# Gate and value products of a SwiGLU kernel: fifteen block products for 2x3x3 blocks in place of seven for 2x2x2

## The chip, the cores and the metric

The kernel runs on one core of a Trainium2 chip. The metric is the device time of one execution in microseconds (us); of the kernel before there are three such times and one profiled execution. The engines are PE (TensorE, matrix products, results in PSUM), DVE (VectorE), ACT (ScalarE), POOL (GpSimd) and SP (SyncE, which here only issues transfers). All data is 32-bit float; an f32 matmul leaves two records in the trace, called passes here.

## The reference

Attention with normalised q and k over 8 sequences of 448 tokens, 12 heads of 64, and behind it a feed-forward part with a SwiGLU. Cut to what matters:

```python
q_n, k_n = rmsnorm(q, g_q), rmsnorm(k, g_k)
attn = softmax(q_n @ k_n^T / sqrt(64))            # per batch and head, 448 x 448
x = concat_heads(attn @ v)                        # 3584 x 768
xn = x / rms(x) * rms_g
g, val = xn @ w_gate, xn @ w_val                  # w_gate, w_val: 768 x 1536
out = (g * sigmoid(g) * val) @ w_out              # w_out: 1536 x 768
```

The weights arrive as 64-bit floats and are turned into 32-bit ones on the chip. The change concerns the two products with `w_gate` and `w_val`, "gate/value" from here on.

## The kernel before

**Order.** `safe_scores` writes the order of the work out by hand: the operations of every engine run in the order in which the program emits them. The main loop goes over 48 pairs of heads, six for each sequence b. A pair has an attention block of seven steps (scores and weighted values on PE, exponentials on ScalarE, their sums on GpSimd), and between the blocks stand the norms, reductions and transposes of the next pairs. `fill` hands out feed-forward "items" from the list `todo` at set places between these: while sequence b is in attention, first the out-projection of b-2, then the gate/value products of b-1 (`begin`). One item is one or a few chains of matmuls with what follows them. `pe(fn)` emits an item and advances the count `now["t"]`; `after(n, fn)` puts an operation n counts later. `LEFT` items at the end of the list are kept for the first block of the next sequence, which hands them out as 2, 1 and 1 around the norms of k. After the last attention block all that remains is emitted without attention work.

**Between two blocks.** `turn` transposes q and k on PE; ScalarE makes qT (L549) from the transposed q and VectorE copies kT (L550). The norms and squares of the next pairs (L530, L493) run on ScalarE in front of qT, their reductions on VectorE.

**Gate/value.** Sequence 0 is done directly (`plain`), while the weights are converted (`convert`) and stored to a DRAM scratch (`kept` for gate and value, `kept_o` for w_out). Sequences 1 to 7 use `quad`: x and the weights are cut into 2x2x2 blocks (224 tokens; inner dimension 384 = 3 chunks of 128; two halves of the columns), and for each of six column pairs of 128 gate and 128 value columns seven products in the order B11, T2, B21, T3, T1, T4, B22 take the place of eight. A product (`product`, matmul in L1081) is 2 (gate, value) x 3 chunks = 6 matmuls of 224 tokens, so a sequence has 252 and the program 1764. The left sides are the blocks A of x and their sums S1 to S4, made by VectorE in `norm_x` (list `slow`, one at a time). The right sides are the raw blocks B and the sums T1 to T4. The results are put together by `plus` (L1093, VectorE, PSUM plus SBUF), after one copy of the first by ScalarE (L1123); twice, a second product is added onto a bank in PSUM that has been read. `hand` makes silu(gate) * value: a tanh on ScalarE (L1100) and, one count later, two operations of VectorE (L1103, L1104, `rest`).

**Weights.** The T blocks are made once, in sequence 1: `derive` (L1003, VectorE) takes two raw blocks that have been loaded, `keep` stores the sum to `kept`, and later sequences load it. An item of column pair fp may not be emitted before all 8 (fp + 1) blocks of its pair and the ones before have been derived (the third number of an item, read in `fill`). `ask` issues the loads in the order of use on SP's queue, as soon as blocks in SBUF are free; there are 23 of them, `w`, and four, `top`, that the conversion leaves. `derive_o` (L1024) makes the 24 sums of w_out's blocks in the same stage, `derive_q` (L1051 to L1054) the two-level sums for the quad out-projection in sequence 2.

**Out-projection.** Sequences 1 and 4 use seven products with w_out (`out_strassen`), sequences 2, 3, 5, 6 and 7 a two-level scheme (`out_quads`), whose left sums are made by `left_q1` (L1248); some of its results are added by GpSimd (L1345). In PSUM the scores have four banks, `ps_m` one, the feed-forward part three (`ps_f`).

Of the kernel before, what the change touches and what calls it, by code (L numbers as in the profile page):

```python
# [25 lines left out]
BW = 384  # L26
# [309 lines left out]
def safe_scores(  # L336
# [25 lines left out]
    NW = 23  # L362
# [3 lines left out]
    x_pool, s_pool, slots = pool("c_x", 4), pool("c_xs", 3), pool("c_slots", 1)  # L366
# [245 lines left out]
    def x_of(g):  # L612

        b, hp = divmod(g, NPAIR)
        half, c = divmod(hp, 3)
        if c == 0 and ("x", b, half) not in st:
            st["x", b, half] = x_pool.tile([128, 3, S], F32, name="x")
        if hp == 0 and ("ss", b) not in st:
            st["ss", b] = tmp.tile([128, S], F32, name="ss", tag="ss", bufs=1)
        return st["x", b, half][:, c, :]  # L620
# [111 lines left out]
    def norm_x(b):  # L732
# [7 lines left out]
        xs = [st["x", b, h] for h in range(2)]  # L740

        def scale(hp):
            x = xs[hp // 3][:, hp % 3, :]
            nc.vector.scalar_tensor_tensor(x, x, rg[:, hp:hp + 1], ps[:, 0:S], ALU.mult, ALU.mult)
# [9 lines left out]
        a = st["left", b] = {f"A{r + 1}{h + 1}": xs[h][:, :, r * HT:(r + 1) * HT] for r in range(2) for h in range(2)}  # L754
        for h in range(2):
            st.pop(("x", b, h))

        def op(name, first, second, what):

            a[name] = a["A21"] if name == "S3" else s_pool.tile([128, 3, HT], F32, name="xs")  # L760
            nc.vector.tensor_tensor(a[name], a[first], a[second], what)

        slow.extend(lambda args=args: op(*args) for args in (("S1", "A21", "A22", ALU.add), ("S2", "S1", "A11", ALU.subtract),
                                                             ("S3", "A11", "A21", ALU.subtract), ("S4", "A12", "S2", ALU.subtract)))
# [4 lines left out]
    def hurry(jobs):  # L769
        while jobs:  # L770
            jobs.pop(0)()

# [10 lines left out]
    kept = scratch.tile([NFP, len(NAMES), 2, 128, BW], F32, name="kept")  # L783
# [18 lines left out]
    free_w = [slots.tile([128, BW], F32, name=f"w{i}") for i in range(NW)]  # L802
# [10 lines left out]
    def block():  # L813
        return free_w.pop(0), free_w

    def room(n):
        return len(free_w) >= n

    def give_back(key):
        t, home = st.pop(key)  # L820
        after(1, lambda: home.append(t))

    def data(key):
        return st[key][0][:, 0:BW]
# [7 lines left out]
    def split(raw, n):  # L832
# [4 lines left out]
        if n < 24 and n % 7 > 3:  # L837

            top = s_pool.tile([128, 3, HT], I32, name="xs")[:, 0:2].rearrange("p c n -> p (c n)")[:, 0:BW]
        else:  # L840
            top = cv_pool.tile([128, BW], I32, name="top")
# [13 lines left out]
    for fc in range(NFC):  # L855
        col, fp = divmod(fc, NFP)
        for w in range(2):
            for half in range(2):
                rows = (moe_w_gate, moe_w_val)[w][half * HALF:(half + 1) * HALF, fc * 128:(fc + 1) * 128]
                pieces.append((("w", 0, fp, BLOCKS[2 * col + half], w), rows.rearrange("(c p) f -> p c f", p=128)))  # L860
# [4 lines left out]
    turn_of = {"n": 0}  # L865
# [3 lines left out]
    def home(key):  # L869
        if key[0] == "w":  # L870
            return kept[key[2], NAMES.index(key[3]), key[4]]
# [5 lines left out]
    def keep(key):  # L877
        nc.sync.dma_start(out=home(key), in_=data(key))

    def convert():  # L880
# [18 lines left out]
        if turn_of["n"] == TURNS:  # L899

            free_w.extend(cv_pool.tile([128, BW], F32, name="top") for _ in range(4))
            whole = [raw_pool.tile([128, 2 * BW], F32, name="raw") for _ in range(7)]
            room_so.extend(whole[:6])
            homes = [whole[6][:, 0:BW], whole[6][:, BW:]] + [cv_pool.tile([128, BW], F32, name="top")[:, :] for _ in range(2)]
# [33 lines left out]
    def raw_q(b):  # L938
        n = sum(key[0] == "wx" for key in uses) // 2
        if n < len(jobs_q):  # L940
            i, j = jobs_q[n]
            uses.extend(("wx", b, ORDER_Q[i], c) for c in (j, j + KG))

    for b in range(1, B):
        for fp in range(NFP):
            for at, name in enumerate(("B12", "B11", "B22", "B21") if b == 1 else ORDER):
                uses += [("w", b, fp, name, w) for w in range(2)]
                if b == 2 and at % 4 == 1:
                    raw_q(b)
            if b == 1:  # L950
                uses += [("wd", b, name, fp) for name in BLOCKS]
        if in_quads(b):
            uses += stream_q(b)
        else:
            for name in ORDER_O:
                for c in range(NFP):
                    uses.append(("wo", b, name, c))
                    if b == 1 and c % 4 == 3 and name not in ORDER_O[:1]:
                        raw_q(2)
                    if b == 1 and c == 1 and name in ORDER_O[-3:]:  # L960
                        raw_q(2)
    assert sum(key[0] == "wx" for key in uses) == 2 * len(jobs_q)
    asked = {"n": 0, "derived": 0}
    derived = [(fp, to, plus, minus, w) for fp in range(NFP) for to, plus, minus in DERIVED for w in range(2)]

    def ask():

        if turn_of["n"] < TURNS:
            return
        while asked["n"] < len(uses):  # L970
            key = uses[asked["n"]]
            keep_free = 4
            if key[1] == 1 and key[0] in ("w", "wd"):
                fp = key[2] if key[0] == "w" else key[3]
                keep_free = max(7 + 8 * fp - asked["derived"], 1)
# [6 lines left out]
            if len(free_w) <= keep_free:  # L982
# [3 lines left out]
            st[key] = block()  # L986
# [3 lines left out]
    def derive(wait=4):  # L990
# [3 lines left out]
        fp, to, plus, minus, w = derived[asked["derived"]]  # L994
        for name in (plus, minus):
            if ("w", 1, fp, name, w) not in st or asked.get(("w", 1, fp, name, w), 0) > now["t"] - wait:
                return False
        if not free_w:
# [742 lines left out]
```

## Time and profile before

| | |
|---|---|
| three executions | 1542.72, 1543.2, 1545.05 us; median 1543.2 |
| profiled execution | 1546.19 us, its span 1544.4, granted clock 0.996 |
| VectorE, ScalarE, GpSimd busy | 60%, 35%, 48% of the span |
| PE, weighted values (L674), scores (L659) | 194.2 us, 233.8 us |
| PE, gate/value products of sequences 1 to 7 (L1081, four groups) | 69.5 + 45.9 + 344.4 + 265.2 us |
| transfers | 327.26 MB, mean 212 GB/s |

A row of a group reads: line, engine, operation, out<-in, shape, count | busy us, mean ns of one | idle us of that engine just before them, and what ended it. "x" and "xs" are the left blocks (raw and summed), "w" and "top" the right ones, "ff" a bank of `ps_f`. A row of the timeline has its start in the span, its length, engine and line, and in brackets the engine's idle time before it with what ended it; runs of like operations are put together (x12). In the windows each engine has its busy time with the number of instructions. Ends of matmuls are modelled by the profiler, so consecutive matmuls overlap in the records, and the time of one is better taken from the distance of starts.

### The profile page before, as it was taken

The numbers are of one execution on the slowest core, as the hardware profiler recorded it, in microseconds if no ns is written. First come the engines' busy times: TensorE is split into PE (matmuls) and PEld (weight loads), VectorE is DVE, ScalarE is ACT, GpSimd is POOL, SyncE is SP. The second block draws the span as 40 slices with busy tenths as digits, with TensorE's granted clock in tenths as the row PEclk, the third lists the DMA queues.
The fourth block names the chain that finished last, engine by engine and source line by source line (L and its number), as shares of the span: only waits on it lengthen the run. The fifth ranks groups of instructions, "written<-read, shape, count | busy, mean of one in ns | idle before, by whom it ended". The sixth has DMA issues, their size and how long they took to land.

```text
span 1544.4 us, 26111 instructions
## 1 busy us (share of the span) xinstructions
PE 1511.2 (98%) x8900; PEld 1187.4 (77%) x8900; DVE 929.8 (60%) x1793; ACT 534.8 (35%) x1241; POOL 736.4 (48%) x718
## 2 busy tenths in 40 slices
PE   8999998999999999999999999999999999999997
PEld 4344444688856888888987888767987889899997
DVE  5788998667754666854457443444458444673464
ACT  6856664333323333234233332424333232101000
POOL 6868887546424354474435652544545731030003
PEclk9999999999999999999999999999999999999998
DMA  7758575776989978886557855584557755577565
GB/s 194 228 153 258 175 228 157 225 229 214 294 274 275 310 253 266 285 250 188 160 163 217 267 176 153 152 275 131 174 155 228 240 160 148 164 256 256 175 194 176
DMA packets 314082, 327.26 MB, mean 212 GB/s; under 512 B 84308, under 2 KB 310868, under 8 KB 313940
## 3 DMA queue, kind: packets, MB, share of 16 engines
q1 hardware_dynamic: 313012, 325.31, 68.1%
q8 instruction: 73, 1.20, 0.3%
q14 instruction: 69, 0.57, 0.1%
q10 hardware_dynamic: 800, 0.20, 0.1%
q0 software_dynamic: 128, 0.00, 0.0%
HBM read 271.62 MB, written 53.77 MB: 211 GB/s over the span
## 4 chain that ended last, share of the span: by engine, by line
PE 83%; DVE 11%; DMA 2%; issue 1%; ACT 1%; POOL 1%; SPq 0%; DVEq 0%; POOLq 0%; ACTq 0%
PE ff L1081 42%; PE ff L1373 10%; PE sc L659 7%; PE av L674 6%; PE ff L1305 5%; PE ff L1440 4%; PE tr L544 2%; PE ff L1178 2%; DVE top L850 1%; DVE top L849 1%; PE den L692 1%; PE den L606 1%; DVE top L848 1%; PE sc L562 1%; DVE l L1248 1%
## 5 line engine op out<-in xcount | busy, mean ns | idle before, releaser
L1081 PE MATMUL ff<-x,w 128*128 128x224 f32 x1686 | 344.4, 354 | 0.0
L1081 PEld LDWEIGHTS ff<-x,w 128*128 128x128 f32 x1686 | 315.2, 190 | 13.2 <-issue 11.3
L1081 PE MATMUL ff<-xs,w 128*128 128x224 f32 x1296 | 265.2, 353 | 2.0 <-DVE w L1003 1.2
L714 POOL TENSOR_TENSOR es<-es,e 128x448 f32<-128x448 f32 x205 | 245.9, 1200 | 13.7
L1081 PEld LDWEIGHTS ff<-xs,w 128*128 128x128 f32 x1296 | 243.9, 190 | 3.4 <-issue 1.5
L659 PE MATMUL sc<-qT,kT 64*64 64x448 f32 x1176 | 233.8, 542 | 5.7 <-ACT e L664 2.9
L674 PE MATMUL av<-e,vt 64*64 64x448 f32 x984 | 194.2, 541 | 0.0
L664 ACT ACTIVATE e<-sc 128x448 f32<-128x448 f32 x294 | 154.4, 547 | 71.4 <-PE sc L659 53.5
L644 POOL TENSOR_TENSOR ss<-ss,rd 128x448 f32<-128x448 f32 x40 | 48.0, 1201 | 218.5 <-ACT rd L643 218.5
L659 PEld LDWEIGHTS sc<-qT,kT 64*64 64x64 f32 x1176 | 79.3, 133 | 87.4 <-issue 61.6
L709 POOL TENSOR_TENSOR es<-e 128x448 f32<-128x448 f32 x41 | 48.2, 1176 | 178.0 <-ACT e L664 178.0
L515 POOL TENSOR_TENSOR rs<-ms,mhalf 128x12 f32<-128x12 f32 (+1 forms) x50 | 115.9, 2319 | 4.2
L1093 DVE TENSOR_TENSOR cc<-ff,u 128x448 f32<-128x448 f32 x84 | 52.3, 623 | 99.6 <-PE ff L1081 99.5
L1440 PE MATMUL ff<-x,w 128*128 128x448 f32 x288 | 111.8, 541 | 0.0
L674 PEld LDWEIGHTS av<-e,vt 64*64 64x64 f32 x984 | 66.2, 133 | 42.4 <-issue 42.4
L1100 ACT ACTIVATE th<-c 128x224 f32<-128x224 f32 x42 | 16.3, 389 | 238.1 <-DVE c L1093 238.1
L1373 PE MATMUL ff<-w,l 128*128 128x192 f32 x500 | 95.6, 329 | 2.8 <-DVE l L1248 2.0
L1440 PEld LDWEIGHTS ff<-x,w 128*128 128x128 f32 x288 | 53.3, 190 | 51.1 <-issue 49.2
L1373 PEld LDWEIGHTS ff<-w,l 128*128 128x128 f32 x500 | 82.6, 190 | 8.1 <-DVE l L1248 3.2
L1345 POOL TENSOR_TENSOR y<-y,c 128x384 f32<-128x384 f32 x10 | 12.2, 1217 | 159.4 <-DVE y L1414 148.0
L1093 DVE TENSOR_TENSOR u<-ff,p 128x448 f32<-128x448 f32 x42 | 26.2, 623 | 84.3 <-PE ff L1081 77.9
L1093 DVE TENSOR_TENSOR u<-ff,u 128x448 f32<-128x448 f32 x42 | 26.1, 623 | 82.6 <-PE ff L1081 82.3
(209 smaller groups left out, 2627.9 us busy)
## 6 DMA issues: line engine op xcount, KB each, us to landing
w<-kept SPq DMA_DIRECT2D x474, 192.0 KB, 3.7
w<-kept_q SPq DMA_DIRECT2D x297, 192.0 KB, 3.8
w<-kept_o SPq DMA_DIRECT2D x132, 192.0 KB, 3.9
kept<-w SPq DMA_DIRECT2D x81, 192.0 KB, 3.9
top<-kept SPq DMA_DIRECT2D x78, 192.0 KB, 3.9
top<-kept_q SPq DMA_DIRECT2D x53, 192.0 KB, 3.2
kept_q<-w SPq DMA_DIRECT2D x52, 192.0 KB, 3.0
qk<-in_q_dram SPq DMA_DIRECT2D x48, 192.0 KB, 3.5
```

Source lines behind the costliest of these rows:

```text
L515: nc.gpsimd.tensor_tensor(st["rs", g][:, cols], ms, mhalf[:, cols], ALU.pow)
L644: after(m, lambda: (nc.gpsimd.tensor_tensor(ss, ss, rd, ALU.add), st.update({("summed", b): hp})))
L659: nc.tensor.matmul(ps[r, 0:S], lhsT=st["kT", g][r, keys_of(i)], rhs=st["qT", g][r, :], start=True, stop=True)
L664: nc.scalar.activation(e, ps[:, 0:S], ACT.Exp)
L674: nc.tensor.matmul(st["av", g][own(j), 0:S], lhsT=vt, rhs=st["e", g, i][r], start=i == 0, stop=i == PARTS - 1, skip_group_check=True)
L709: nc.gpsimd.tensor_tensor(st["es", g], st["e", g, 0], st["e", g, 1], ALU.add)
L714: nc.gpsimd.tensor_tensor(st["es", g], st["es", g], st["e", g, i], ALU.add)
L1081: nc.tensor.matmul(bank[:, w * HT:(w + 1) * HT], lhsT=wt[:, c * 128:(c + 1) * 128], rhs=x[:, c, :], start=onto is None and w == c == 0, st ...
L1093: nc.vector.tensor_tensor(add[name], ps[:, 0:S], add[other], ALU.add)
L1305: nc.tensor.matmul(ps, lhsT=left_o(b, which, LEFT_O[name], c), rhs=data(("wo", b, name, c)), start=first and c == 0, stop=c == NFP - 1, sk ...
L1373: nc.tensor.matmul(ps, lhsT=a[:, j, :], rhs=data(key)[:, n % 2 * HW:(n % 2 + 1) * HW], start=start and j == 0, stop=j == KG - 1, skip_grou ...
L1440: nc.tensor.matmul(bank[w][:, 0:S], lhsT=data(key)[:, c * 128:(c + 1) * 128], rhs=st["x", 0, half][:, c, :], start=half == c == 0, stop=ha ...
```

## The change

Gate and value of sequences 1 to 7 use fifteen products for 2x3x3 blocks (`three`): tokens 2 x 224, inner dimension 3 x 256 (2 chunks of 128), and a group of columns 3 x (128 gate + 128 value); there are four such groups, taken in the order 0, 2, 1, 3. The direct way has 18 products. A product is 2 x 2 = 4 matmuls of 224, a sequence 60 products.

```diff
+    LEFT_G = {"S3": ("a21", "a23", ALU.add), "S6": ("a23", "a22", ALU.subtract), "S8": ("a11", "a12", ALU.subtract),
+              "S9": ("a13", "a21", ALU.add), "S4": ("a13", "S6", ALU.subtract), "S5": ("a21", "S8", ALU.subtract),
+              "S2": ("a12", "S4", ALU.subtract), "S0": ("a22", "S5", ALU.subtract), "S1": ("a23", "a13", ALU.subtract),
+              "S13": ("a11", "a21", ALU.subtract), "S12": ("a11", "a13", ALU.add)}
+    RIGHT_G = {"v9": ("b11", "b33", None), "v4": ("b21", None, "b32"), "v5": ("b12", None, "b23"),
+               "v1": ("b21", "b33", "b31"), "v14": ("b12", "b21", "b22"), "v11": ("b22", "b23", "b32"),
+               "v10": ("b13", "b12", "-b33"), "v13": ("b13", "b11", "b23"), "v7": ("b31", "b11", "-b32")}
+    PRODUCTS = (("q3", "S3", "b33"), ("q6", "S6", "b32"), ("q8", "S8", "b12"), ("q9", "S9", "v9"), ("q4", "S4", "v4"),
+                ("q5", "S5", "v5"), ("q7", "a13", "v7"), ("q2", "S2", "b21"), ("q0", "S0", "b23"), ("q1", "S1", "v1"),
+                ("q14", "a12", "v14"), ("q11", "a22", "v11"), ("q12", "S12", "b11"), ("q10", "a21", "v10"), ("q13", "S13", "v13"))
```

Left sums: 11 operations of 448 per sequence in place of four of 672; one that isn't made yet is made in front of its product. The results are chained in three banks, B, X and Y: the next product is added onto a bank that ScalarE has copied out, without a new start. In the order of the products: q3 into B, q6 X, q8 Y, q9 onto B, q4 onto X, q5 onto Y, q7 B, q2 X, q0 Y, q1 B, q14 X, q11 Y; q12 into a new bank Z, q10 into another, q13 onto Z.

```diff
+        def copy(name, ps):
+            nc.scalar.copy(T[name], ps[:, 0:S])
+        def plus(name, ps):
+            nc.vector.tensor_tensor(T[name], ps[:, 0:S], T[name], ALU.add)
+        def more(name, one, other, what):
+            nc.gpsimd.tensor_tensor(T[name], T[one], T[other], what)
...
+        def q5(make):
+            T["pc"] = pair("pc")
+            T["c13"], T["c23"] = T["pc"][:, 0], T["pc"][:, 1]
+            copy("c13", make(bank["Y"]))
+            more("c13", "c13", "s", ALU.add)
+            more("c13", "c13", "d", ALU.subtract)
...
+        def q11(make):
+            plus("c22", make(bank["Y"]))
+            after(1, lambda: hand("pa", 1, 1))
+        def q12(make):
+            bank["Z"] = make()
+            plus("c11", bank["Z"])
+            after(1, lambda: hand("pb", 0, 2))
+        def q10(make):
+            ps = make()
+            plus("c23", ps)
+            plus("c13", ps)
+        def q13(make):
+            if n == len(GROUPS) - 1 and in_quads(b):
+                after(1, lambda: left_q1(b, 0, range(3)))
+            plus("c13", make(bank["Z"]))
+            after(1, lambda: hand("pc", 2, 1))
```

In each group ScalarE copies after q3, q6, q8, q9, q4, q5, q7, q2 and q0 (nine "snapshots", 252 in all; before, 42 copies), GpSimd makes five sums (140 in all), VectorE seven `plus` (196, before 210), and three `hand` of 448 each finish two column blocks of both token halves (84 tanh in place of 126).

Derived right blocks: nine per group, 15 operations of 512 (60 in all, before 48 of 384), one block per item, and an item may be emitted as soon as the block that it uses itself has been derived; so the derivation of a block may stand one or two items in front of its product. When all are made, `derive_o` runs twice per item, and the first item of a block name in the out-projection of sequence 1 forces what is still missing.

```diff
+    derived = [(g, to) for g in GROUPS for _, _, to in PRODUCTS if to in RIGHT_G]
...
+                made += b == 1 and right in RIGHT_G
+                items.append((4 * HT, TURNS, (made, ("wg", b, g, right)), fn))
...
+            made, key = sums_made or (0, None)
+            while asked["derived"] < made or (key and key not in st):
+                before = dict(asked)
                 derive(0)
+                if key and key[0] == "wo":
+                    derive_o(0)
                 ask()
-                if n == asked["derived"]:
+                if before == asked:
                     pe(idle)
...
             if now["t"] - st["block"] > 4 and now["t"] != st.get("left_sums"):
-                left = 3 - sum(derive() for _ in range(3))
-                for _ in range(left):
+                if not derive():
                     derive_o()
-                for _ in range(2):
-                    derive_q()
+                derive_o()
+                derive_q()
```

Weights in SBUF: a gate/value block is 128 x 512 (gate and value together, 256 KB). The 23 single blocks become an arena of 22 x 384 columns in places of 128; gate/value blocks take four places from its start, others three from its end, and 18 places are kept for the raw blocks of `derive_o` and `derive_q` (`side`, loaded in their own order) until `derive_q` is through. A load is issued only if more than three further blocks of its kind find room (two for the raw blocks of sequence 1).

```diff
+            kind, keep_free = "wg" if key[0] == "wg" else "w", 3
+            if key[1] == 1 and key[0] == "wg":
+                keep_free = 2
...
-            if len(free_w) <= keep_free:
+            if not room(keep_free + 1, kind):
                 return
```

Converted blocks of gate and value are stored as three pieces of 128 columns. In the quad out-projection the sum for B22 (ten operations of 384) goes from GpSimd to VectorE. The pools of x, its sums and the temporaries are cut anew. Since an item is smaller now, `LEFT` is 10 in place of 7, and they are handed out as 3, 2 and 1:

```diff
-    AHEAD, LEFT = 20, 7
+    LEFT = 10
...
+        fill(3)
+        norm_k(g + 1, 0)
         fill(2)
-        norm_k(g + 1, 0)
-        fill(1)
         pe(lambda: turn(g + 1, 0))
```

The program has 10507 matmuls where it had 10591; the other shapes of matmul keep their numbers. SP issues 1831 transfers in place of 1999.

## The prediction

> **What bounds the kernel now.** I read the page from the top, then the windows of the gate/value stages, then timelines around single products, then the groups by line and the waits of VectorE. First the page:
>
> ```profile
> PE 1511.2 (98%) x8900; PEld 1187.4 (77%) x8900; DVE 929.8 (60%) x1793; ACT 534.8 (35%) x1241; POOL 736.4 (48%) x718
> ...
> PE 83%; DVE 11%; DMA 2%; issue 1%; ACT 1%; POOL 1%; SPq 0%; DVEq 0%; POOLq 0%; ACTq 0%
> ...
> L1081 PE MATMUL ff<-x,w 128*128 128x224 f32 x1686 | 344.4, 354 | 0.0
> ...
> L1081 PE MATMUL ff<-xs,w 128*128 128x224 f32 x1296 | 265.2, 353 | 2.0 <-DVE w L1003 1.2
> ...
> w<-kept SPq DMA_DIRECT2D x474, 192.0 KB, 3.7
> ```
>
> TensorE is busy 98% of the span at a granted clock of 0.996, so work taken from it shortens the kernel only as far as no new wait appears. The two L1081 rows are the gate/value products; before them PE idled 2.0 us in all, 1.2 behind a derived block. Two smaller rows read blocks from another buffer; each f32 matmul leaves two records, so 1764 matmuls are 3528 passes.
>
> The windows show the stage of sequence 1, where the derived weights are made, and a stretch of the last stage with nothing but products:
>
> ```profile
> core 0: us, PE busy (x) PEld busy (x) DVE busy (x) ACT busy (x) POOL busy (x), PEclk, DMA share, GB/s
> 320.00:450.00 130.00, 128.83 (x772) 102.82 (x765) 92.10 (x183) 47.48 (x114) 65.04 (x58) 1.00 0.76 244
> 1400.00:1425.00 25.00, 25.00 (x134) 25.00 (x133) 8.24 (x17) 3.16 (x7) 0.00 (x0) 1.00 0.74 229
> ```
>
> In the second, a pass takes 25/134 = .187 us. Over all gate/value stages the median distance between starts of passes is .189, which I use. VectorE has 71% of the first stretch, the fullest of its stages.
>
> **Removed from TensorE.** 84 matmuls go, 168 passes: 168 × .189 = **−31.8**. By the mean of the busy time (69.5+45.9+344.4+265.2 = 725 us over 3528 passes, .2055, with overlaps counted twice) it is −34.5; by .1866, −31.3. A product is now 8 passes, 1.51 us, where it was 12, 2.27.
>
> **Work added to the others.** The rows that price it:
>
> ```profile
> L1003 DVE TENSOR_TENSOR w<-w,w 128x384 f32<-128x384 f32 x23 | 11.9, 549 | 0.0
> L1024 DVE TENSOR_TENSOR w<-w,w 128x384 f32<-128x384 f32 x22 | 15.4, 702 | 0.4
> L1103 DVE SCALAR_TENSOR_TENSOR h<-th,cc 128x448 f32<-128x448 f32 x42 | 26.4, 629 | 0.7 <-ACT th L1100 0.7
> L1104 DVE SCALAR_TENSOR_TENSOR h<-h,cc 128x448 f32<-128x448 f32 x42 | 27.1, 645 | 1.4
> L1123 ACT COPY p<-ff 128x448 f32<-128x448 f32 x42 | 22.4, 532 | 121.7 <-PE ff L1081 94.1 <-POOL c L1345 27.6
> L714 POOL TENSOR_TENSOR es<-es,e 128x448 f32<-128x448 f32 x205 | 245.9, 1200 | 13.7
> ```
>
> ScalarE: 210 more copies × .532 = +112, less 42 tanh × .389 or less. GpSimd: 140 adds × 1.20 = +168, less ten that move away. VectorE: 60 derived steps instead of 48; a 512-wide step I take at .68 (192 columns .35–.44, 384 .55–.70, so .16–.2 per further 128). By these counts VectorE goes from 956 to 979 us, ScalarE 598 to 705, GpSimd 746 to 903: none becomes the bound over the whole. In sequence 1's gate/value, PE falls from 126 to 122 us and VectorE rises from 93 to 109; that is cover enough on average, and the price comes from order, below.
>
> [...]
>
> ```profile
> L638 DVE TENSOR_TENSOR x<-av,rd 128x448 f32<-128x448 f32 x28 | 17.4, 621 | 2.2 <-PE av L674 1.1
> L638 DVE TENSOR_TENSOR x<-x,rd 128x448 f32<-128x448 f32 x20 | 17.3, 864 | 0.7
> ```
>
> (621 with one input in PSUM, 864 with both in SBUF.) [...]
>
> **Waits in sequence 1's gate/value.** Each derived block is now made one or two products ahead of its use, by VectorE, and behind operations that wait for TensorE themselves. Nothing else is in front of PE then: it stands, and with it the score matmuls queued behind. The timeline gives the handover:
>
> ```profile
> 549.13 0.62 DVE L1093 TENSOR_TENSOR cc<-ff,u 128x448 f32<-128x448 f32 x1
> 549.67 0.61 DVE L1093 TENSOR_TENSOR c<-ff,u 128x448 f32<-128x448 f32 x1
> ...
> 549.80 2.54 PE L1081 MATMUL ff<-xs,w 128*128 128x224 f32 x12 [0.80 <-DVE cc L1093]
> ...
> 552.38 0.62 DVE L1093 TENSOR_TENSOR cc<-ff,u 128x448 f32<-128x448 f32 x1 [1.63 <-PE ff L1081]
> ```
>
> The product that starts at 549.80 ends at 549.80 + 12 × .189 = 552.07; VectorE starts on it .31 later; a second 448-wide sum starts .54 after the first; PE follows the end of a VectorE sum (549.75) by .05.
> - First column group: four products in a row, each with a left sum (.61), a derived step (.68) and an out-projection sum (.70), ask VectorE 2.0 us against PE's 1.51. Worked through operation by operation, q9 waits 2.0 and q5 1.5.
> - First group, q13: its block v13 is emitted behind two sums on q10's result and the pair of the first `hand`: .31 + two sums 1.08 + pair (L1103, L1104) 1.27 + two dependent steps 1.40 + .05 = 4.1.
> - Second group, q13: the same, with the copy of kT (L550, which waits for qT, shown below) and reductions in front: 5.0.
> - Third group: q7 2.3, q11 3.2, and q10, q13 and the next q6 and q9 .4–.7 each, 2.3.
> - Fourth group: q14 1.2, q11 .7, q10 1.0, q13 .8: 3.7.
>
> Sum 24.1, less the 1.2 that is there already: **+23**. Low: only the two q13 and half of the rest, 12; high: the rest half as dear again and the 512-wide step at .86, 32.
>
> **Waits in the out-projection of sequence 1.** The blocks T2 of w_out are stored to DRAM and loaded back when all 24 sums are made. The last four (c=5) are now forced just in front of their first use. In front of them on VectorE stands the copy of kT, which waits for qT of ScalarE, which is behind three norms and two squares:
>
> ```profile
> DVE kT L550 <- ACT qT L549: 61.7, 33, 4.0
> ```
> ```profile
> 1058.61 0.81 ACT L530 ACTIVATE qk<-qk,rs 128x64 f32<-128x64 f32 x3
> ...
> 1059.32 0.93 ACT L493 ACTIVATE sq<-qk 128x384 f32<-128x384 f32 x2
> ...
> 1061.06 0.63 ACT L549 ACTIVATE qT<-tr,gqk 128x448 f32<-128x448 f32 x1 [0.81 <-PE tr L548]
> ```
>
> From the end of PE's work: .31 + a copy .48 + norms .7 + squares .8 + qT .6 = 3.0; reductions .9; four sums 2.0; store and issue .45; landing 3.0–3.9 (192 KB take 3.7 in the page's row): 9.4–10.2, less transposes of .9 that run meanwhile: **+9**. Low, without the queue in front: sums and landing, less what PE has left, 4.4. High: store and load after each other, 11.
>
> **Smaller ones.** Start of sequence 2's gate/value: its first block is asked for one product before use: landing 3.7 less 1.5, and issue behind the others 1.2: **+3.4** (1 to 6). Starts of out-projections of sequences 2, 3, 5, 6, 7: `left_q1` now stands behind the last pair of `hand` (1.27, of which .45 is hidden): **+4** (0 to 8). Chains in PSUM: the next product on a bank comes two products (3.02) after the last; a snapshot needs .31 + .53, so ScalarE's exps between may take 2.2 us before PE waits; where four exps of .55 stand in front it is even: **+1** (0 to 10). Loads: a gate/value block is 256 KB, fewer are held, and the shortest lead is 4.9–5.5 us at the starts of sequences 3, 4, 6, 7 against a landing of 3.7–3.9: **+3** (0 to 8).
>
> At nothing: the last sums of the quad out-projections (B22, ten of 384) go from GpSimd (1.22 each) to VectorE (.55), which has room there; two of them lie at the kernel's end, so −1.3 at best. `LEFT` 10 and the fills of 3, 2, 1 hand out 4.5, 3.0 and 1.5 us where 2, 1, 1 products of 2.27 were 4.5, 2.3 and 2.3: the same cover, and .8 less for the last turn if it were short. The stores of converted weights are three pieces of the same bytes.
>
> **Sum.** −31.8 + 23 + 9 + 3.4 + 4 + 1 + 3 = **+11.6**. Against the profiled execution (1546.19, span 1544.4 and 1.8 around it) 1557.8; that execution is 3 above the median, so **1555** by the median. All low ends: −34.5 + 12 + 4.4 + 1 = −17, 1526. All high ends: −31.3 + 32 + 11 + 6 + 8 + 10 + 8 = +44, 1587.
>
> **Rivals.**
> - *Faster, the waits stay short.* For: the one wait for a derived block that the trace has is small, 1.17 us:
>
> ```profile
> 361.71 1.37 PE L1081 MATMUL ff<-xs,w 128*128 128x224 f32 x6 [1.17 <-DVE w L1003]
> ```
>   Ten such places cost 12, the out-projection 4.4, the small ones 4: −31.8 + 20.4 = −11.4, **1532**. It decides from where sequence 1's gate/value waits less than 11.4 us in all (31.8 less the other terms as summed above, 9 + 3.4 + 4 + 1 + 3). Against: in that trace the block was not behind a sum of the product just before; here v13 is, every time.
> - *ScalarE's snapshots hold PE in every stage.* For: nine per group, 252 in all, each in front of a product on its bank. If 35 blocks of exps each cost .4, +14 to +15: **1570**. Against: ScalarE is 35% busy and gets 3.02 us.
> - *Transfers bind.* For: the DMA share is .76 already in sequence 1, and fewer blocks are held. Ten late loads of 1 us: +10, **1565**. Against: fewer transfers in number (1999 issues on SP's queue become 1831).
> - That TensorE's work does not fall can be left out: the program lists 10507 matmuls instead of 10591, the other shapes unchanged.
>
> **Chances.** My forecast (waits in sequence 1 and its out-projection eat the gain, 1541–1572) .52; faster .28; snapshots .12; transfers .08. About 0.2%, 3 us, is what a measurement of this kernel can tell from no change: that band (1540–1546) takes .06 of the forecast's low end and .01 of the first rival. So faster .28, same .07, slower .65. The range 1530–1576 leaves out the fast part of the first rival and the slow tail of the snapshots.
>
> **What would show it.** Products at .189 per pass with 168 passes fewer; in sequence 1, PE waits of 4–5 us before q13 of the first two groups, put down to VectorE's derived steps, and some 20 us of PE idle there; a wait of 9–10 us for a DMA at the first T2 product of its out-projection. Wrong, if the derived steps come out on time (VectorE waiting for blocks, not PE for VectorE), if PE idles instead before the products that follow a snapshot, or if its idle time lies at the starts of stages with a DMA named.

## The result, and the profile after

The changed kernel takes 1614.68 us (median of 4 runs, 1613.91 to 1617.44) beside 1543.05 of the kernel before: a ratio of 1.0465, 95% interval 1.0446 to 1.0483, 72 us slower. The profiled execution has a span of 1612.4 us, 68.0 more than before.

The page of the changed kernel:

```profile
PE 1508.5 (94%) x8732; PEld 1170.4 (73%) x8732; DVE 981.7 (61%) x1766; ACT 639.6 (40%) x1409; POOL 898.2 (56%) x848
...
PEclk9999999999988999999999999999999999999999
...
L1162 PE MATMUL ff<-x,w 128*128 128x224 f32 x1344 | 278.6, 362 | 20.5 <-DVE w L1075 12.4
...
L1183 POOL TENSOR_TENSOR pc<-pc,l 128x448 f32<-128x448 f32 x84 | 98.7, 1175 | 254.2 <-ACT pc L1177 231.2
...
w<-kept SPq DMA_DIRECT2D x396, 256.0 KB, 3.7
```

PE has 168 passes fewer and is busy 2.7 us less in a span 68 us longer: the time went into waiting and into slower work. The clock row has two slices of 8 where only the last one was below 9 before, at 443 to 524 us: the end of the stage in which the derived weights are made, and the out-projection behind it. The waits of VectorE, ScalarE and GpSimd do not matter by themselves; those of PE do. The list of PE's waits (line waited for, total, times, longest):

```profile
PE ff L1162 <- DVE w L1075: 26.2, 11, 6.7
PE ff L1425 <- DMA w<-kept_o: 9.4, 3, 8.5
PE ff L1496 <- issue: 8.7, 5, 2.0
PE msx L725 <- POOL ss L643: 7.7, 5, 1.9
PE ff L1162 <- DVE pb L1180: 7.5, 6, 1.5
```

L1075 is the second step of a derived block, L1425 the out-projection of sequences 1 and 4, L725 the matmul on the sums of squares in front of an out-projection, L1496 the quad out-projections, L1180 the `plus` of a gate/value group. The windows by stage (gate/value of sequence 1; its out-projection with the wait at the start of sequence 2; gate/value of 2, of 3, of 7):

```profile
294.10:460.10 166.00, 135.72 (x769) 112.75 (x767) 121.95 (x182) 60.56 (x134) 93.91 (x82) 0.91 0.52 168
460.10:545.50 85.40, 71.51 (x303) 38.58 (x303) 37.40 (x77) 18.50 (x43) 23.35 (x23) 0.94 0.64 200
545.50:679.40 133.90, 124.53 (x761) 105.18 (x762) 83.38 (x157) 57.64 (x125) 77.03 (x72) 0.98 0.92 287
746.60:867.60 121.00, 118.03 (x754) 101.19 (x754) 51.05 (x93) 57.18 (x124) 79.16 (x76) 1.00 0.58 179
1463.10:1552.40 89.30, 89.30 (x474) 89.30 (x473) 32.42 (x57) 24.67 (x46) 23.30 (x23) 1.00 0.66 201
```

The lengths, taken between the first products of each stage, before and after: 125.7 and 166.0; 67.7 and 85.4; 124.7 and 133.9; 121.3 and 121.0; 93.1 and 89.3. The first two stages of the kernel before, in the same form:

```profile
296.50:422.20 125.70, 124.53 (x793) 108.11 (x791) 91.22 (x176) 46.00 (x111) 69.40 (x64) 1.00 0.77 250
422.20:489.90 67.70, 67.70 (x304) 37.47 (x303) 36.78 (x84) 18.63 (x43) 23.63 (x24) 1.00 0.88 269
```

Where nothing but products runs (sequence 7) the gain of 3.8 is there; in sequence 3 it is used up; sequence 1 alone, with its out-projection, loses 58.

### The profile page after: what moved, and what is told of

It reads as the page before. It is cut to its first block, busy times and chain, and to the rows that moved or that the text cites. A ratio compares the mean times of both kernels' runs of the same rounds, so it can differ in the third digit from the quotient of the medians.

```text
span 1612.4 us, 25793 instructions
## 1 busy us (share of the span) xinstructions
PE 1508.5 (94%) x8732; PEld 1170.4 (73%) x8732; DVE 981.7 (61%) x1766; ACT 639.6 (40%) x1409; POOL 898.2 (56%) x848
## 5 line engine op out<-in xcount | busy, mean ns | idle before, releaser
L1162 PE MATMUL ff<-x,w 128*128 128x224 f32 x1344 | 278.6, 362 | 20.5 <-DVE w L1075 12.4
L1162 PEld LDWEIGHTS ff<-x,w 128*128 128x128 f32 x1344 | 258.1, 195 | 28.9 <-issue 10.2
L1183 POOL TENSOR_TENSOR pc<-pc,l 128x448 f32<-128x448 f32 x84 | 98.7, 1175 | 254.2 <-ACT pc L1177 231.2
L1162 PE MATMUL ff<-xs,w 128*128 128x224 f32 x896 | 181.5, 358 | 8.8 <-DMA w<-kept 4.7
L1162 PEld LDWEIGHTS ff<-xs,w 128*128 128x128 f32 x896 | 170.6, 194 | 13.9 <-issue 7.7
L1180 DVE TENSOR_TENSOR pb<-ff,pb 128x448 f32<-128x448 f32 x56 | 34.8, 621 | 189.7 <-PE ff L1162 187.0
L1496 PE MATMUL ff<-w,l 128*128 128x192 f32 x630 | 119.0, 330 | 14.7 <-issue 8.7
L1496 PEld LDWEIGHTS ff<-w,l 128*128 128x128 f32 x630 | 103.4, 190 | 22.0 <-issue 12.1
L1162 PE MATMUL ff<-top_x,w 128*128 128x224 f32 x448 | 93.0, 357 | 3.1 <-DVE w L1075 2.0
L1162 PEld LDWEIGHTS ff<-top_x,w 128*128 128x128 f32 x448 | 83.1, 190 | 15.2 <-issue 12.3
L1564 PEld LDWEIGHTS ff<-x,w 128*128 128x128 f32 x288 | 53.8, 192 | 51.6 <-issue 49.6
L1162 PE MATMUL ff<-l,w 128*128 128x224 f32 x448 | 89.7, 353 | 0.0
```

The source lines that it names most:

```text
L1162: nc.tensor.matmul(bank[:, w * HT:(w + 1) * HT], lhsT=data(key)[:, (2 * w + c) * 128:(2 * w + c + 1) * 128], rhs=a[left][:, c, :], start=o ...
L1180: nc.vector.tensor_tensor(T[name], ps[:, 0:S], T[name], ALU.add)
L1183: nc.gpsimd.tensor_tensor(T[name], T[one], T[other], what)
L1496: nc.tensor.matmul(ps, lhsT=a[:, j, :], rhs=data(key)[:, n % 2 * HW:(n % 2 + 1) * HW], start=start and j == 0, stop=j == KG - 1, skip_grou ...
L1564: nc.tensor.matmul(bank[w][:, 0:S], lhsT=data(key)[:, c * 128:(c + 1) * 128], rhs=st["x", 0][:, 3 * half + c, :], start=half == c == 0, st ...
```

## What a wait costs: the clock

Two windows of the stage of sequence 1, around and right behind the end of the first long wait:

```profile
330.00:337.00 7.00, 6.35 (x19) 5.77 (x20) 3.52 (x8) 1.81 (x5) 0.00 (x0) 0.52 0.36 123
337.00:344.00 7.00, 7.00 (x40) 6.95 (x40) 6.90 (x14) 2.75 (x6) 5.60 (x6) 1.00 0.47 174
```

PE is busy in both; in the first it does 19 passes at a granted clock of 0.52, in the second 40 at 1.00. The prediction has no term of this kind, so it was measured by itself, with waits put into the kernel before:

```diff
+        if (fp, right) == (3, "B21"):
+            for _ in range((0, 0, 1, 2, 3, 5, 8, 12)[b]):
+                nc.vector.tensor_scalar(x[:, :, 0:192], x[:, :, 0:192], 1.0, None, ALU.mult)
```

> The kernel before with one wait put into each of the sequences 2 to 7: 1, 2, 3, 5, 8 and 12 multiplications by 1.0 of VectorE on the left block of the product with B21 in column pair 3. Waits of some 1.7, 2.5, 3.3, 4.9, 7.3 and 10.5 us of TensorE, 30 in all. Theory 'a wait is paid twice': windows of half the granted clock follow the waits of about 3 us and more, 3.4 to 10 us long each, and the time grows by the waits plus 8 to 16: 1581-1590. Rival 'a wait costs what it lasts': no windows, 1543 + 30 = 1570-1576.

1592.5 us beside 1548.85 of the kernel before, one execution each. The waits of PE in the timeline ("issue": the profile names nothing; PE waits for the multiplications that were put in front of the product):

```profile
557.07 2.51 PE L1084 MATMUL ff<-x,w 128*128 128x224 f32 x12 [2.49 <-issue]
747.87 2.58 PE L1084 MATMUL ff<-x,w 128*128 128x224 f32 x6 [3.88 <-issue]
941.70 3.70 PE L1084 MATMUL ff<-x,w 128*128 128x224 f32 x9 [4.48 <-issue]
1117.73 2.58 PE L1084 MATMUL ff<-x,w 128*128 128x224 f32 x6 [7.32 <-issue]
1313.98 3.32 PE L1084 MATMUL ff<-x,w 128*128 128x224 f32 x8 [7.45 <-issue]
1485.44 2.95 PE L1084 MATMUL ff<-x,w 128*128 128x224 f32 x7 [9.02 <-issue]
```

| wait, us | stretch of half clock, us | stage longer by, us |
|---|---|---|
| 2.49 | none | 2.9 |
| 3.88 | 6.83 | 6.6 |
| 4.48 | 6.83 | 7.6 |
| 7.32 | 6.83 | 9.5 |
| 7.45 | 10.24 | 10.5 |
| 9.02 | 10.24 | 11.7 |

The waits sum to 34.6, the stages grow by 48.8 (the span by 46.3, as this execution reached sequence 1 2.5 us earlier). Here the wait of 2.49 us costs about what it lasts, those from 3.88 on 2 to 3 us more, about half of that part of the stretch which lies outside the wait. The stretches are two and three times 3.41 us long here, one to three times in the changed kernel. There a shorter wait was enough: one of 1.94 us and one of .61 just behind it were followed by 3.41 us of half clock.

The traces show more. In each of them the stretches start at whole multiples of 3.413 us from one another (in the changed kernel at 329.92, 370.88, 405.01, ...). If the time at full clock, from 290 us on to the last gate/value product, is cut into pieces on this grid, the 14 profiles have 4904 of them. All 60 in which PE has 2.0 us or more without a matmul record are followed by half clock, 17 of the 53 with 1.5 to 2.0 us are, and 1 of the 4791 with less. The wait of 2.49 us lies across a border of the grid, .54 on one side and 1.95 on the other; waits of 1.97 and 1.71 that fall into one piece almost whole were followed by half clock in the changed kernel.

From the start of sequence 1's gate/value to the last of the gate/value products the changed kernel has 54.6 us of such stretches, the kernel before none. 10.8 us of them lie within waits; the other 43.8 at half speed are an estimate of 22 us lost.

## Why PE waits in sequence 1

The first long wait is the one that the prediction puts before q13 of the first group. VectorE and PE there:

```profile
325.41 0.62 DVE L1180 TENSOR_TENSOR pb<-ff,pb 128x448 f32<-128x448 f32 x1 [0.89 <-PE ff L1162]
326.93 1.15 DVE L1180 TENSOR_TENSOR pc<-ff,pc 128x448 f32<-128x448 f32 x2 [0.89 <-PE ff L1162]
328.00 0.62 DVE L1194 SCALAR_TENSOR_TENSOR h<-th,pa 128x448 f32<-128x448 f32 x1
328.65 0.62 DVE L1195 SCALAR_TENSOR_TENSOR h<-h,pa 128x448 f32<-128x448 f32 x1
329.19 0.68 DVE L1072 TENSOR_TENSOR w<-w 128x512 f32<-128x512 f32 x1
329.91 0.69 DVE L1075 TENSOR_TENSOR w<-w 128x512 f32<-128x512 f32 x1
```
```profile
330.65 0.74 PE L1162 MATMUL ff<-raw,w 128*128 128x224 f32 x1 [3.83 <-DVE w L1075]
```

Two sums on q10's result, the pair of `hand`, two derived steps, then the product: 3.83 us, predicted 4.1. But other steps took twice as long as these. A little earlier, beside GpSimd's sums of exponentials:

```profile
317.62 1.52 DVE L1075 TENSOR_TENSOR w<-w 128x512 f32<-128x512 f32 x1
319.07 0.61 DVE L1180 TENSOR_TENSOR pb<-ff,pb 128x448 f32<-128x448 f32 x1
319.61 1.09 DVE L1072 TENSOR_TENSOR w<-w 128x512 f32<-128x512 f32 x1
320.73 1.51 DVE L1075 TENSOR_TENSOR w<-w 128x512 f32<-128x512 f32 x1
```
```profile
318.68 6.98 POOL L713 TENSOR_TENSOR es<-es,e 128x448 f32<-128x448 f32 x5
```

Of the 60 derived steps 40 took .68, the others 1.44 on average; 19 of those 20 lie beside 448-wide sums of GpSimd. The `plus` between them has one input in PSUM and keeps its .61. The sums of L637 in this profile (L638 in the kernel before) did the same: with both inputs in SBUF they took 1.46 to 1.53 us in the 6 cases beside 448-wide operations of GpSimd and .62 to .79 in the other 14, with one input in PSUM never more than .63. In all the derived steps took 56.2 us instead of 60 × .68 = 40.8: 15 more. The prediction adds them up at .68 each. The .24 by which its two rows of L638 differ (864 and 621 ns) would make 14 over 60 steps; that the totals meet is luck, as 20 steps took some .76 more.

Eight runs take the stage apart, one execution each. Lengths of stages in us, from the traces (s1, s2, s3: gate/value of sequences 1 to 3; o1: out-projection of sequence 1 up to the first product of sequence 2), and the time of each beside the kernel before on the same chip:

| kernel | s1 | o1 | s2 | s3 | time | before |
|---|---|---|---|---|---|---|
| before | 125.7 | 67.7 | 124.7 | 121.3 | | 1543.05 |
| changed | 166.0 | 85.4 | 133.9 | 121.0 | 1614.68 | 1543.05 |
| derived block in front of the item | 175.8 | 80.4 | 132.5 | 121.0 | 1620.23 | 1548.85 |
| snapshot of q7 apart | 165.9 | 83.4 | 136.2 | 122.8 | 1612.43 | 1548.85 |
| no derived steps | 126.4 | 84.1 | 136.4 | 122.2 | 1581.76 | 1548.85 |
| derived, not waited for | 143.6 | 79.3 | 139.1 | 121.0 | 1594.19 | 1545.71 |
| no GpSimd sums | 160.1 | 84.5 | 129.9 | 117.5 | 1589.65 | 1545.71 |
| sequence 1 direct | 139.0 | 67.7 | 133.5 | 122.7 | 1571.69 | 1545.71 |
| the same, sums on VectorE | 139.1 | 67.7 | 132.8 | 117.8 | 1554.36 | 1545.71 |
| derived also behind attention blocks | 151.3 | 79.7 | 132.5 | 121.0 | 1593.43 | 1546.2 |

**No derived steps.** In sequence 1 the first raw block of each stands in for the sum:

```diff
-            nc.vector.tensor_tensor(t, at, parts[minus], ALU.subtract)
...
-            nc.vector.tensor_tensor(t, at, parts[plus.lstrip("-")], ALU.subtract if plus[0] == "-" else ALU.add)
+        t = data(("wg", 1, g, first))
```

> The changed kernel without the 60 steps on VectorE that make the derived right blocks: in sequence 1 the first raw block of each stands in for the sum (the products and the stores stay). Theory 'derived blocks late': the gate/value stage of sequence 1 falls from 166.0 to 122-128 us and no slow-clock window stays in it; the whole falls by 38-46, to 1569-1577. Rival 'snapshots and GpSimd's sums hold TensorE there as in sequence 2': the stage keeps 134 or more, as the stage of sequence 2 does, the whole above 1582.

126.4: the derived blocks cost 39.6 us of the stage. The whole is 5 above the expected range. Sequence 2 keeps its waits; it and its out-projection take 5.4 us more than in the changed kernel, with 17.1 us of half clock in place of 6.8: nearly the same waits (4.78 and 1.94 us) have 6.83 us of it behind them here and 3.41 there.

**Derived, but not waited for.** The steps stay, the products of sequence 1 take the raw block:

```diff
-        key = ("wg", b, g, right)
+        key = ("wg", b, g, RIGHT_G[right][0] if b == 1 and right in RIGHT_G else right)
```

> The changed kernel with all 60 derived steps of sequence 1 kept and stored, but its products take the first raw block of each in place of the derived one, so that TensorE does not wait for the steps; VectorE and GpSimd do the same work. Theory 'lead': the stage falls from 166.0 to within 4 us of what it took without the steps (126.4). Rival 'load': VectorE's steps push its sums and the copies of kT back, and the stage stays at 140 or more.

143.6, between the two: of the 39.6 us 22.4 come with PE waiting for the block itself, 17.2 with the load alone. PE stands 17.4 us here, 4.3 without the steps; 7.5 are put down to VectorE's sums and a copy of kT, 4.5 to ScalarE, 2.7 to GpSimd's sum of squares. The windows of these two runs, stage of sequence 1 (without the steps, then with them):

```profile
294.30:420.70 126.40, 122.08 (x769) 104.84 (x768) 72.09 (x122) 60.39 (x134) 86.48 (x80) 0.99 0.72 235
```
```profile
294.50:438.10 143.60, 126.21 (x769) 105.62 (x768) 128.18 (x182) 60.49 (x134) 95.23 (x80) 0.98 0.64 206
```

The third busy time is VectorE's: 72 us without and 128 with the steps, 89% of the stage. The prediction counted 109 of 122.

**The order alone.** First the block was put in front of the item's own sums:

```diff
+            early = now["t"] + 1 - st["block"] > 4 and derive()
             pe(fn)
...
-                if not derive():
+                if not early:
```

> The changed kernel, but in sequence 1 the derived right block of an item is emitted in front of that item's own product and sums, not behind them; nothing else moves. Theory 'order' (TensorE stands because the derived block is queued on VectorE behind sums that wait for TensorE): the waits of 4.0 and 6.7 us before q13 of the first two groups go, and with them the slow-clock windows behind them (6.8 us each at half the clock, some 3.4 lost each); the gate/value stage of sequence 1, 166.0 us now, falls to 145-152, the whole to 1594-1601. Rival 'VectorE is full' (its steps take 1.5 us beside GpSimd's sums where they take .68 alone, so the wait only moves): the stage keeps over 160, the whole stays above 1608.

1620.23: a wait of 3.84 stands before q13 of the first group as before, and one of 6.80 in the second group, before q10, one product earlier. The run does not decide: the program makes no derived block within four counts of an attention block, so v13 of the first group was still made behind the same two sums and pair, and other blocks came later than before (a wait of 3.65 before q7). The next run lifts that bar:

```diff
-            if now["t"] - st["block"] > 4 and now["t"] != st.get("left_sums"):
-                if not derive():
+            made = st["block"] < now["t"] != st.get("left_sums") and derive()
+            if now["t"] - st["block"] > 4 and now["t"] != st.get("left_sums"):
+                if not made:
```

> The changed kernel, but derived blocks of sequence 1 may also be made in the items right behind an attention block (before, not within four counts of it); nothing else. v13 of the first two groups is then emitted four items ahead of q13 and not one, most others two to four. By the run in which TensorE does not wait for the steps (143.6, against 166.0) and the one without the steps (126.4), lead is worth 22 us and VectorE's load 17. Theory: the stage falls to 143-150, the waits of 4.0 and 6.9 before q13 go, the whole falls to 1590-1600; the wait of 8.7 at the first T2 product stays. Rival 'the steps now hold the attention's own work on VectorE': waits move to the score products, the stage stays above 157.

151.3: of the waits before the first two q13 one is gone and one is .65; in their place are waits of 2.95, 2.77 and 5.78 elsewhere in the stage, and one of 4.76 for GpSimd's sum of squares. 14.7 us gained of the 22.4 that lead is worth.

**Without GpSimd's sums.**

```diff
-            nc.gpsimd.tensor_tensor(T[name], T[one], T[other], what)
+            pass
```

> The changed kernel without the 140 sums that GpSimd makes from the snapshots (five per group; nothing in their place). Two theories on them. 'They slow VectorE': of the 60 derived steps those that run beside 448-wide sums of GpSimd took 1.1 to 1.6 us, alone .68; without them most fall to .7 and the gate/value stage of sequence 1, 166.0 us, to under 152. 'They come too late': the plus of q12 and with it the copy of kT and the bank of q13 wait for them; then the stage of sequence 2, 133.9, falls to 122-126, sequences 3 and 4 from 121.0 to 117-118. If neither, both stages keep their lengths to within 3 us and only the order of the derived blocks is left.

Sequence 1 keeps 160.1, 5.9 less. The steps do get faster: 57 of the 60 take .69, and all together 43.3 us, 13 less than in the changed kernel. But the waits before the first two q13 stay (3.77 and 6.82). So GpSimd's sums slow the steps, and the slow steps are a small part of what the stage loses. Sequences 3 and 4 fall to 117.5, as expected; sequence 2 falls by 4 only, and two of its last waits (.81 and 2.29) are now for transfers.

## GpSimd's queue in sequences 2 to 6

In sequence 2 of the changed kernel, GpSimd, ScalarE, VectorE and PE:

```profile
629.21 1.25 POOL L708 TENSOR_TENSOR es<-e 128x448 f32<-128x448 f32 x1
630.54 1.14 POOL L713 TENSOR_TENSOR es<-es,e 128x448 f32<-128x448 f32 x1
631.63 1.25 POOL L1183 TENSOR_TENSOR l<-pc,l 128x448 f32<-128x448 f32 x1
632.96 1.13 POOL L1183 TENSOR_TENSOR pb<-pb,l 128x448 f32<-128x448 f32 x1
```
```profile
632.91 0.53 ACT L1177 COPY pc<-ff 128x448 f32<-128x448 f32 x1 [3.09 <-POOL l L1183]
```
```profile
635.54 0.22 DVE L550 COPY kT<-tr 128x64 f32<-128x64 f32 x1 [3.65 <-ACT qT L549]
...
636.60 0.61 DVE L1180 TENSOR_TENSOR pb<-ff,pb 128x448 f32<-128x448 f32 x1
```
```profile
637.27 3.29 PE L1162 MATMUL ff<-x,w 128*128 128x224 f32 x16 [1.53 <-DVE pb L1180]
```

GpSimd's five sums stand between its sums of exponentials (1.2 us each); ScalarE waits to overwrite the snapshot of q7 until GpSimd has read it; qT comes late, with it the copy of kT, the `plus` behind that, and the bank which the next product needs. The same queue delays the sum of squares before an out-projection (`PE msx` in the list of waits). To cut the chain at ScalarE, q7's snapshot was put elsewhere, into one of the two buffers that the tanh uses:

```diff
-            copy("c23", make(bank["B"]))
-            more("d", "c23", "d", ALU.subtract)
+            T["q7"] = tmp.tile([128, S], F32, name="th", tag="th", bufs=2)
+            copy("q7", make(bank["B"]))
+            more("d", "q7", "d", ALU.subtract)
```

> The changed kernel, but q7's snapshot goes into a buffer of its own, so that ScalarE's copy of q0 need not wait until GpSimd has read the one of q7. Theory 'the queue of GpSimd holds ScalarE, the copy of kT, VectorE and the bank': ScalarE's 29 us of waiting for GpSimd's sum go, the waits of 1.0 to 2.0 us before the last products of a group in sequences 2, 3 and 4 (10.6 in sequence 2) go for the most part; the gate/value stage of sequence 2, 133.8 us, falls to 124-127, the whole by 8 to 14. Rival 'GpSimd's sum itself comes too late for VectorE': the waits keep their places, the whole stays within 3 us of 1614.

No gain: 1612.43, sequence 2 at 136.2, its long wait (2.59) still behind VectorE's `plus`. ScalarE's 29.1 us of waiting for GpSimd's sum are gone, so they did not hold PE. This speaks for the rival: GpSimd's sum itself is late. Moving the sums was tried together with the next edit.

**Sequence 1 by the direct 18 products**, three chained in a bank and read from there by `hand`, no left sums; the derived blocks are made in the same stage and only stored:

```diff
+    STEPS = [(j, i, k) for j in COLUMNS for i in (1, 2) for k in (1, 2, 3)]
...
+            bank[j, i] = product(b, g, f"a{i}{k}", f"b{k}{j}", bank.get((j, i)))
+            if k == 3:
+                hand(j, i)
```

> The changed kernel, but sequence 1 makes gate and value by the 18 direct products per group (raw blocks only, three products chained in a bank, 48 matmuls more); the derived blocks are made and stored for the later sequences, and nothing in sequence 1 waits for them. Theory 'a derived block one item ahead of its product': the stage loses its waits and windows of slow clock and pays 96 passes of .189 = 18 us: 166.0 becomes 138-143. The sums of w_out's blocks are through earlier, so the wait of 8.7 at the first T2 product and the one of 4.8 at the start of sequence 2 shrink: 85.4 becomes 68-78. Whole 1572-1584. Rival 'VectorE is full there': the stage stays above 150.

139.0 and 67.7. The stage is bound by PE again (waits of .8 in all), with 48 matmuls more; the w_out sums are made in time, and the waits of 8.5 us for their blocks and of 4.7 at the start of sequence 2 are gone. Then the sums of sequences 2 to 7:

```diff
-            nc.gpsimd.tensor_tensor(T[name], T[one], T[other], what)
+            nc.vector.tensor_tensor(T[name], T[one], T[other], what)
```

> As the run with sequence 1 direct, and the five sums per group of sequences 2 to 7 (120 in all) made by VectorE in place of GpSimd. Theory 'GpSimd's queue is what holds sequences 2 to 6': the stage of sequence 2 falls from 134 to 121-125, those of 3 and 4 from 121.0 to 117-118.5, the wait of 1.7 to 1.9 at the sum of squares before each out-projection goes; whole 12 to 25 below the run before it: 1552-1568. Rival 'VectorE's queue takes its place': waits before the products of q10 to q13 and the next q3 as long as before, no gain of 5.

1554.36, the span 17.4 below that of the run before it. Sequences 3 and 4 are at 117.8; sequence 2 stays at 132.8, now by waits for transfers (2.02, 1.67) and for a copy of kT (2.67).

## Was there a version faster than the kernel before?

Three more kernels have both of these edits, and two others. `keep_free` is raised to 5 for w_out while `derive_q` runs and lowered to 2 for sequence 2, and `left_q1` moves from q13 to q14 of the last group:

```diff
+            if todo_q and key[0] == "wo":
+                keep_free = 5
+            if todo_q and key[:2] == ("wg", 2):
+                keep_free = 2
...
+            if n == len(GROUPS) - 1 and in_quads(b):
+                after(1, lambda: left_q1(b, 0, range(3)))
```

> As the run with sequence 1 direct and the sums on VectorE (1554), with two more edits: the loads leave more blocks free while the two-level sums of w_out are made (so that these start in the out-projection of sequence 1, and the blocks of sequence 2 are asked for at least five items ahead), and the first left sums of a quad out-projection stand four products earlier. Expected: sequence 2's stage 132.8 to 125-129, each of five out-projections 1.5 us less; whole 1538-1546, that is 0.995 to 1.001 of the kernel before. Rival 'the transfers of sequence 2 bind' (their share is .95): its stage stays above 131, whole 1547 or more.

1548.49 beside 1546.2: a ratio of 1.0018 (1.0005 to 1.0030). Sequence 2 is at 129.6, each quad out-projection 1.5 to 2.2 shorter (67.0 to 65.3 in sequence 2). With fifteen products in all sequences, and derived blocks and w_out's sums made behind attention blocks too:

> The changed kernel with fifteen products in every sequence, the snapshots' sums on VectorE, derived blocks and w_out's sums also made right behind attention blocks, and the two edits of the run beside it. Sums of w_out are through 30 items before the T2 products (before: in the item in front of them), so the wait of 8.7 us and its slow clock go: 85.4 becomes 68-70. Sequence 1's stage is the question: VectorE's load with 20 sums more, but GpSimd lighter and the steps not slowed: theory 'lead' 126-140, whole 1526-1545; rival 'load' 145-155, whole 1548-1560.

1567.75, a ratio of 1.0148 (1.0131 to 1.0165): sequence 1 at 156.4, and 76.9 for its out-projection, where the wait for T2 is down to 1.2 but one of 3.87 for VectorE brings 6.83 us of half clock. Stage and whole are above what even the rival "load" expected, though only 12 of the 60 steps are slow. Of the 25.3 us that PE stands in sequence 1, 13.7 are still put down to derived blocks, so the run does not separate lead from load. Sequence 2 is at 125.2. And with sequence 1 direct and the same lift (`keep_free` 4 for w_out):

> As the run with sequence 1 direct and more lead (1548.5, 1.002 of the kernel before), but derived blocks and w_out's sums may be made right behind attention blocks too, and one block fewer is left free for the two-level sums; these start at item 234 in place of 257 and end at 340 in place of 362 of the program, so fewer of their transfers and steps fall into sequence 2's gate/value. Expected: sequence 2's stage 129.6 to 124-127 (125.2 in the run with fifteen products and the same lift), the out-projection of sequence 1 70.1 to 68-69: whole 1540-1545, 0.996-0.999 of before. Rival 'their transfers now meet those of sequence 1's out-projection, whose DMA waits grow': whole unchanged, 1547 or more.

1552.12, a ratio of 1.0038 (1.0023 to 1.0053). The steps behind the attention block now hold a copy of kT (a wait of 4.90 us with 6.83 of half clock): 145.6 in sequence 1. Sequence 2 does not fall either: 130.5 where 124 to 127 was expected, with a wait of 3.57 for a transfer near its start. None of the three is faster than the kernel before; the best gives back 15 us in sequence 1 for the products that it saves in the others.

## Why the prediction was wrong

It said slower, by 11.6 and at most 44; it was 68 by the spans. Term by term:

- **168 passes, −31.8**: right where PE is alone (93.1 to 89.3 in sequence 7).
- **Sequence 1's gate/value, +23 (12 to 32)**: the mechanism was right and most waits stood where they were put (3.83 for 4.1, 6.73 for 5.0 before the two q13). The derived blocks cost 39.6. PE stood 30.1 us in the stage where 24.1 were added up. One step that failed is "VectorE rises from 93 to 109; that is cover enough on average": it was busy 122 there, and its load alone cost 17.2. (The low end does not follow from its words: the two q13, 9.1, and half of the rest, 7.5, less 1.2 are 15.4, not 12.)
- **A wait costs what it lasts**: never written down, but in every term, and a second step that failed. The stage of sequence 1 has four stretches of half clock, 30.7 us together, 5.7 of them within waits: an estimate of 12.5 us lost. With the 28.9 us of waits more than before these are 41 of the 44.8 by which the stage exceeds 121.2. The out-projection has one stretch of 10.24, sequence 2's start one of 3.41.
- **T2, +9, and the start of sequence 2, +3.4**: waits of 8.51 and 4.68, well sized; with the clock 17.7.
- **GpSimd, +168 of busy time, "none becomes the bound over the whole"**: priced at nothing, a third step that failed. Taking the sums off it in sequences 2 to 7 gained 17.4. A queue that is busy for 56% of the span was late where its sums stood between the sums of exponentials.
- **`left_q1`, +4**: five waits of 1.5 to 2.0. Moving it (together with the edit of `keep_free`) took 1.7 us off three out-projections, 1.5 off the fourth, 2.2 off the end: 8.7.
- **Transfers, +3**: at the starts of sequences 3, 4, 6 and 7, for which this term was meant, no product waited for a block. They show in sequence 2 once GpSimd's sums are gone: the best version lies 9.4 us above 120.2 there (124.7 less a seventh of the gain), and 5.1 of its waits are for loads.
- **Snapshots on ScalarE, +1**: about right; one wait of PE, of 1.2 us, is put down to them in the changed kernel.

The losses found, 39.6 + 17.7 + 17.4 + 8.7 + 9.4, and 5.2 that sequence 1 keeps without its steps (126.4 against 121.2), make 98.0; less 31.8 that is 66 of the 68. They come from runs of different kernels, so that the sum comes out so close is no proof of its parts. Cut by the stages of the two profiles alone, the 68.0 are +40.3 in sequence 1's gate/value, +17.7 in its out-projection, +9.2 in sequence 2's gate/value, +10.8 in the five quad out-projections, −7.5 in the gate/value stages of sequences 3 to 7 with the out-projection of 4, and −2.4 before sequence 1. Of the rivals, "faster" fell at the point that was named (11.4 us in sequence 1); "snapshots" had the right stages and the wrong engine: the sums behind the snapshots, on GpSimd, not the copies. "Transfers" has only the 4.7 us at the start of sequence 2 for it, which the forecast had priced.

## What to carry to other kernels

PE was 98% busy here, and the exchange of matmuls for sums was lost above all in the one stage in which the sums are made and used at once, and right behind it (58 of the 68 us). Look at lead (blocks made several products ahead) and load there, not over the span. Price each wait of PE of about 4 us and more with 2 to 3 us on top (those of 3.88 to 9.02 us cost 2.2 to 3.1 more than they lasted), and expect half clock behind a shorter one too when PE stands 2 us within one piece of 3.41 (it followed in all 60 cases). And count sums of VectorE with two SBUF inputs at their slow duration (1.44 us on average here, .68 otherwise, for 512 columns) wherever GpSimd has 448-wide sums at the same time; here that was worth at most the 5.9 us by which the stage fell without GpSimd's sums.

## What the runs showed that was not expected

- Half clock after waits, on a grid of 3.413 us, in all 60 cases of the 14 profiles in which PE stood 2.0 us or more within one piece of it; together 54.6 us of stretches in the changed kernel.
- A 512-wide sum of VectorE with both inputs in SBUF takes .68 us alone or beside GpSimd's small operations, 1.1 to 1.6 in the 19 cases beside its 448-wide sums; a 448-wide one with an input in PSUM keeps .62 in both cases.
